# Decays by channel, a two-factor solve, wider MLP matmuls and a pacing scheduler in a fused RWKV-7 and MLP kernel

## The chip, the cores and the metric

One core of a Trainium2 chip runs the whole program. The metric is the device time of one execution in microseconds, as the median of several. Everything is fp32.

## The reference

A recurrence over 768 time steps for 4 batches of 8 heads of width 40, and an MLP on its output, with tokens as rows:

```python
for t in range(S):
    y[:, :, t] = np.einsum('bhd,bhde->bhe', rt, state)
    Sa = np.einsum('bhde,bhe->bhd', state, at)
    state_decay = state * wt[:, :, None, :] - np.einsum('bhd,bhe->bhde', Sa, bt)
    state = state_decay + np.einsum('bhd,bhe->bhde', vt, kt)
x = attn_out.transpose(0, 2, 1, 3).reshape(B * S, H * D)   # 3072 x 320
h = x @ w_in                                               # 320 -> 2048
g = h * (1.0 / (1.0 + np.exp(-1.702 * h)))
out = g @ w_out                                            # 2048 -> 320
```

`w_in` and `w_out` arrive as 64-bit floats and are converted in the kernel.

## The kernel before

**Units.** Time is cut into 12 chunks of 64 steps. A unit `i` is one chunk of two batches (16 heads), so there are 24 units; unit `i` needs the state that unit `i - 2` leaves. All matmuls work on quarters of the array: four 64x64 pieces, `QUARTERS`, each with its own 64 partitions of operands and of results. One `mm` in the code is one quarter, and an fp32 `mm` is two MATMUL and two LDWEIGHTS instructions in the profile.

**One unit.** `cum` multiplies the logarithms of the decays by triangles, which gives cumulative sums; `session` takes `Exp` of them (F, G and `wch`, and the `Ln` of the next chunk's decays, for two units at once). `prep` scales a, b and k by these, by time; `turned` transposes the three by matmuls with the identity (`ps_turn`, L487) and copies them back; the scores N, its transpose and A follow, each with a mask on VectorE, then A times v. `solve` adds the incoming state (`ah_z`, `ps_ahZ`) and solves (I - N) X = X0 in six levels (L592). A level holds W = [N | X | N transposed] for 16 heads in two halves b. Its matmuls square N, square its transpose, multiply X, and add X again by a matmul with the identity (L608); then one copy brings all from PSUM to the next W (L613). The last level keeps X alone. After it come the state's update (`ps_Z`), the transpose of the solution (`ps_saT`), the readout (`ps_rz`, `ps_M`, `ps_y`) and the transposed output xT (`ps_xT`), from which the MLP starts.

**The MLP.** For each chunk (256 tokens) `up` makes 8 tiles g of 256 hidden channels, 5 products of 256 columns each, with the activation on ScalarE; `down` makes two tiles of 128 tokens from 16 products of 320 columns each.

**PSUM.** Its eight banks are four pairs. Every group of matmuls takes a pair, and gives it back when its result has been read.

**Order.** Everything is a task of the class `Plan`, with a rank, its engines and their costs in ns, and what it reads and overwrites. `order` simulates the engines and writes out one order for all: of the tasks that are able to start, each engine takes the lowest rank. The recurrence has ranks around 10 i, the conversion of the weights 5000 and more, the MLP 10000 and more. `fits` says whether a PSUM pair is to be had: the MLP (`most=2`) may hold two and must leave one clear. `fetched` holds a model of instruction fetch on TensorE, 256 instructions in 3750 ns; where a task would wait over 100 ns for it, `order` looks for another task that would not. Each engine then executes its tasks in that order, and waits on semaphores. Buffers have the slots given at L198; a task that writes slot n waits for the users of the contents before.

Of the kernel before, what the change touches and what calls it, by code (L numbers as in the profile page):

```python
# [17 lines left out]
FP32 = mybir.dt.float32  # L18
# [37 lines left out]
class Plan:  # L56
# [4 lines left out]
    BLOCK, FETCH = 256, 3750.0  # L61
# [30 lines left out]
    def order(self):  # L92
# [84 lines left out]
def rwkv7_gelu_quick(ctx: ExitStack, tc: tile.TileContext, time_d, w_d, chan_d, w_in, w_out, out):  # L177
# [10 lines left out]
    LEVELS = 6  # L188
    HALF = [slice(0, 64), slice(64, 128)]
# [7 lines left out]

    plan = Plan(dict(in_w=4, logw=4, F=4, G=4, wch=4, wz=2, in_time=2, in_chan=3, kh=3, bh=3, ah=2,  # L198
                     ahT=2, khT=2, bhT=2, A=1, Av=2, RV=2, W=3, zraw=2, z=2, zT=2, sa=2, saT=1, M=1,
                     rz=1, y=1, x=2, xT=4, g=10, ob=1, raw=4, scale=2), 4)  # L200
# [49 lines left out]
    def triangle(name, compare, sign):  # L250

        t = single(name, [128, 64])
# [5 lines left out]
        return t  # L258


    incl = triangle("incl", ALU.is_ge, 1)
    excl = triangle("excl", ALU.is_gt, 1)
    halves = single("halves", [128, 2])
    nc.vector.memset(halves[:, 0:1], 0.0)
    nc.vector.memset(halves[:, 1:2], 1.0)
    for p in HALF:
        q = slice(p.start, p.start + MID)
        nc.vector.tensor_scalar_add(incl[q], incl[q], -1.0)
        nc.vector.tensor_scalar_add(excl[q], excl[q], -1.0)
        nc.vector.memset(halves[q, 0:1], 1.0)  # L270
        nc.vector.memset(halves[q, 1:2], 0.0)
    upper = triangle("upper", ALU.is_gt, 1)
    lower = triangle("lower", ALU.is_gt, -1)

    def mask(t):
# [3 lines left out]
    padded = {name: [single(f"{name}{i}", [128, 8, 64]) for i in range(plan.slots[name])]  # L279
              for name in ("kh", "bh", "ah", "z")}  # L280
    for ts in padded.values():
        for t in ts:
            nc.gpsimd.memset(t[:, :, D:], 0.0)
    sa = [single(f"sa{i}", [128, 2, 2, 2, 64]) for i in range(2)]
    for t in sa:
        nc.gpsimd.memset(t, 0.0)
    wch = [single(f"wch{i}", [128, 2, 2, 2, 2]) for i in range(4)]
    for t in wch:
        nc.vector.memset(t, 0.0)

    def kept(name, i):
        return padded[name][i % plan.slots[name]]
# [10 lines left out]
    def raws(n):  # L303
        q = n // 2
        if ("raw", q) not in tiles:
            tiles["raw", q] = work.tile([128, 2, DM], INT64, tag=f"xT{2 + q % 2}", name="raw")
        return tiles["raw", q][:, n % 2]

    def weight(n, key, dst, *srcs):
        P, cols = dst.shape  # L310
        rank = 5000 + n

        place = (n // 2) % 2
        raw = lambda: raws(n)[:P, :cols]
        word = lambda dt, w: raw().bitcast(dt).rearrange("p (n two) -> p n two", two=2)[:, :, w]
        scale = lambda: buf("scale", n, [128, 2, DM], INT32)[:P, 0, :cols]
        frac = lambda: buf("scale", n, [128, 2, DM], INT32)[:P, 1, :cols]

        def fetch(t):
            for i, src in enumerate(srcs):  # L320
                to = raw()[i * P // len(srcs):(i + 1) * P // len(srcs)]
                nc.sync.dma_start(to if len(src.shape) == 2 else
                                  to.rearrange("p (m f) -> p m f", m=src.shape[1]), src)
# [4 lines left out]
        def bounded(t):  # L328

            nc.gpsimd.tensor_scalar(scale().bitcast(FP32), scale().bitcast(FP32), low, high, ALU.max, ALU.min)  # L330
# [7 lines left out]
        def value(t):  # L338

            nc.vector.tensor_scalar(frac(), word(INT32, 1), 0xFFFFF, 0x100000, ALU.bitwise_and, ALU.bitwise_or)  # L340
            nc.vector.scalar_tensor_tensor(dst, in0=word(UINT32, 0), scalar=2.0 ** -32, in1=frac(),
                                           op0=ALU.mult, op1=ALU.add)
            nc.vector.scalar_tensor_tensor(dst, in0=dst, scalar=2.0 ** -20, in1=scale().bitcast(FP32),
                                           op0=ALU.mult, op1=ALU.mult)

        ns = 60.0 + 1.4 * cols
        here = dict(uses=[("xT", place - 2)])
        plan.add(15 + n * 0.4, {"SP": 60.0 * len(srcs)}, fetch, writes=[("raw", n)], size=P * cols * 8)
        plan.add(rank, {"DVE": ns}, magnitude, reads=[("raw", n)], writes=[("scale", n)], **here)
        plan.add(rank, {"POOL": 4.8 * cols}, bounded, reads=[("scale", n)], writes=[("bounded", n)])  # L350
        plan.add(rank, {"DVE": 2 * ns}, exponent, reads=[("raw", n), ("scale", n), ("bounded", n)], writes=[("exponent", n)], **here)
        plan.add(rank, {"DVE": 3 * ns}, value, reads=[("raw", n), ("scale", n), ("exponent", n)], writes=[key], **here)

    def weights():
        blocks = w_in.rearrange("(k p) (m r f) -> k r p m f", p=64, r=2, f=128)
        n = 0
        for m in range(0, NM, 2):
            for k in range(NK):
                weight(n, ("w_in", (m // 2, k)), w_in_sb[:, k, m:m + 2].rearrange("p m f -> p (m f)"),
                       blocks[k, 0][:, m:m + 2], blocks[k, 1][:, m:m + 2])  # L360
                n += 1
        for f in range(NF):
            weight(n, ("w_out", f), w_out_sb[:, f, :], w_out[f * 128:(f + 1) * 128, :])
            n += 1


    in_time = lambda i: buf("in_time", i, [128, 5, DM])
    in_chan = lambda i: buf("in_chan", i, [128, 2, 8, 64])
    in_w = lambda i: buf("in_w", i, [128, DM])
    logw = lambda i: buf("logw", i, [128, DM])  # L370

    def load_w(i):
        plan.add(10 * i - 20, {"SP": 60.0}, lambda t: nc.sync.dma_start(in_w(i), w_d[i]),
                 writes=[("in_w", i)], size=128 * DM * 4)

    def load(i):
        plan.add(10 * i, {"SP": 60.0}, lambda t: nc.sync.dma_start(in_time(i), time_d[i]),
                 writes=[("in_time", i)], size=128 * 5 * DM * 4)
        plan.add(10 * i, {"SP": 60.0}, lambda t: nc.sync.dma_start(in_chan(i), chan_d[i]),
                 writes=[("in_chan", i)], size=128 * 1024 * 4)  # L380
# [3 lines left out]
    G_of = lambda i: buf("G", i, [128, 2, 160])  # L384

    def cum(i):
        def go(t):
            ps, lw = psum(t, "ps_cum"), logw(i)
            for b in BITS:
                for n in BITS:  # L390
                    u = b ^ n
                    mm(ps[HALF[u], b, :160], incl[HALF[b]], lw[HALF[b], n * 160:(n + 1) * 160], True)
            for b in BITS:
                mm(ps[HALF[b], b, 160:480], excl[HALF[b]], lw[HALF[b]], False)
            for f in BITS:
                for n in BITS:
                    for b, e in QUARTERS:
                        u = b ^ n
                        o, h = 480 + 4 * u + 2 * f, head(e, f, b, u)
                        mm(ps[e * 64:e * 64 + D, b, o:o + 2], lw[HALF[b], h * D:(h + 1) * D], halves[HALF[b]], False)  # L400
        plan.add(10 * i - 9, pe((1, 160), (1, 320), (4, 2)), go, reads=[("logw", i)],
                 writes=[("cum", i)], room=[("F", i), ("G", i), ("wch", i)], pair=("cum", i))

    def session(c):

        now = [2 * c, 2 * c + 1] if c >= 0 else []
        nxt = [i for i in (2 * c + 2, 2 * c + 3) if i < NU]

        def exps(i):
            def go(t):  # L410
                if i == now[0]:
                    nc.scalar.preload_act_table_set("natural_log_exp_and_others")
                ps, w = psum(t, "ps_cum"), wch[i % 4]
                nc.scalar.activation(G_of(i), ps[:, :, :160], ACT.Exp, scale=-1.0)  # L414
                for b in BITS:
# [439 lines left out]
```

## Time and profile before

| | |
|---|---|
| median of 3 runs | 1110.31 us (1108.95 to 1114.78) |
| the profiled execution | 1109.09 us, its span 1107.4 us |
| TensorE busy, matmuls | 912.8 us, 32,416 MATMUL |
| VectorE / ScalarE / GpSimd busy | 319.1 / 366.4 / 81.5 us |
| costliest groups | `ps_up` 251.7 us, `ps_down` 232.8 us, `ps_level` 232.3 us and 121.2 us with the identity |
| first and last `ps_up` | 121.4 and 1085.3 us |
| first and last `ps_down` | 277.6 and 1102.4 us |
| last `ps_xT` of the recurrence | 947.4 us |

The busy time of the matmuls is the time in which at least one is in flight; four quarters run beside each other, and a matmul lasts longer than the distance to the next one. So a busy share says little of how full the array is; the number of MATMULs in a stretch of time says more.

### The profile page before, as it was taken

The page shows a single profiled execution, that of the slowest core. Times are in us where ns is not written, and L with a number is a line of the kernel's source. Part 1 is how long each engine was busy: PE and PEld are TensorE (multiplying, and loading weights), DVE is VectorE, ACT ScalarE, POOL GpSimd, SP SyncE. Part 2 cuts the span into 40 slices and gives each one's busy share as a digit, 9 for nine tenths or more (in the row PEclk, how much of TensorE's full clock was granted, in tenths as well). Part 3 has the DMA queues.
Part 4 walks back from the last instruction along what each step waited for, and adds up shares of the span by engine and source line. Part 5 has one row for each costly group of instructions (what it writes and reads, how often), then busy time and mean ns, then how long its engine had stood idle before and what let it go on. Part 6 is the DMA issues. An engine that isn't in the chain of part 4 may idle for free.

```text
span 1107.4 us, 67140 instructions
## 1 busy us (share of the span) xinstructions
PE 912.8 (82%) x32416; PEld 754.1 (68%) x32416; DVE 319.1 (29%) x688; ACT 366.4 (33%) x663; POOL 81.5 (7%) x115
## 2 busy tenths in 40 slices
PE   7566787756887777987768988688988999999998
PEld 6556676656676666777667867677877866666664
DVE  4686666322423224123132131320231200000000
ACT  4333433443335333243342344333244221111211
POOL 3322322100000000000010010000010000000000
PEclk8998989999999999999999999999999999999999
DMA  6333433201211011011111111201100000000000
GB/s 204 109 105 85 134 105 95 65 4 53 70 54 54 21 53 65 27 48 59 53 46 35 47 59 34 65 17 40 58 4 10 4 14 14 14 8 8 15 14 13
DMA packets 22542, 54.89 MB, mean 50 GB/s; under 512 B 2816, under 2 KB 14080, under 8 KB 22272
## 3 DMA queue, kind: packets, MB, share of 16 engines
q1 hardware_dynamic: 22272, 50.61, 14.8%
q8 instruction: 253, 4.15, 1.6%
q14 instruction: 17, 0.14, 0.0%
HBM read 46.66 MB, written 3.93 MB: 46 GB/s over the span
## 4 chain that ended last, share of the span: by engine, by line
PE 79%; issue 16%; DVE 2%; ACT 1%; DMA 0%; POOL 0%; SPq 0%; DVEq 0%; POOLq 0%; ACTq 0%
PE ps_up L739 19%; PE ps_down L758 19%; PE ps_level L219 18%; PE ps_turn L219 3%; PE ps_cum L219 2%; PE ps_y L219 2%; PE ps_N L219 2%; PE ps_Z L219 2%; PE ps_xT L219 1%; PE ps_saT L219 1%; PE ps_RV L219 1%; PE ps_Av L219 1%; PE ps_M L219 1%; PE ps_A L219 1%; PE ps_rz L219 1%
## 5 line engine op out<-in xcount | busy, mean ns | idle before, releaser
L219 PE MATMUL ps_level<-W 64*64 64x64 f32 (+2 forms) x8448 | 232.3, 236 | 61.3 <-issue 56.5
L219 PEld LDWEIGHTS ps_level<-W 64*64 64x64 f32 x8448 | 215.5, 137 | 77.4 <-issue 65.6
L739 PE MATMUL ps_up<-xT,w_in_sb 64*64 64x256 f32 x3840 | 251.7, 382 | 19.3 <-issue 17.2
L758 PE MATMUL ps_down<-w_out_sb,g 64*64 64x320 f32 x3072 | 232.8, 433 | 4.3 <-issue 4.1
L613 ACT COPY W<-ps_level 128x672 f32<-128x672 f32 (+1 forms) x220 | 148.7, 684 | 220.7 <-PE ps_level L219 214.2
L739 PEld LDWEIGHTS ps_up<-xT,w_in_sb 64*64 64x64 f32 x3840 | 160.5, 135 | 68.4 <-issue 28.6
L758 PEld LDWEIGHTS ps_down<-w_out_sb,g 64*64 64x64 f32 x3072 | 129.8, 134 | 70.4 <-issue 10.1
L219 PE MATMUL ps_level<-W,ident 64*64 64x80 f32 x2304 | 121.2, 238 | 8.2 <-issue 8.2
L745 ACT ACTIVATE g<-ps_up 128x512 f32<-128x512 f32 x96 | 57.4, 598 | 127.4 <-PE ps_up L739 126.4
L219 PEld LDWEIGHTS ps_level<-W,ident 64*64 64x64 f32 x2304 | 87.6, 138 | 10.2 <-issue 10.2
L769 DVE TENSOR_TENSOR ob<-ob,ps_down 128x320 f32<-128x320 f32 x24 | 11.7, 488 | 211.0 <-ACT ob L766 211.0
L766 ACT COPY ob<-ps_down 128x320 f32<-128x320 f32 x24 | 10.2, 426 | 127.5 <-PE ps_down L758 127.5
L330 POOL TENSOR_SCALAR scale<-scale 128x256 f32<-128x256 f32 (+1 forms) x36 | 41.3, 1160 | 116.0 <-DVE scale L326 116.0
L468 POOL TENSOR_TENSOR ah<-in_time,F 128x320 f32<-128x320 f32 x14 | 12.7, 904 | 360.5 <-ACT F L416 347.8
L473 POOL TENSOR_TENSOR kh<-in_time,G 128x320 f32<-128x320 f32 x18 | 16.6, 922 | 243.9 <-ACT G L414 146.2
L219 PE MATMUL ps_y<-kh,RV 64*64 64x40 f32 x768 | 28.8, 232 | 4.8 <-issue 4.8
L219 PE MATMUL ps_y<-bh,M 64*64 64x40 f32 x768 | 29.0, 235 | 4.0 <-issue 3.7
L613 DVE COPY W<-ps_level 128x416 f32<-128x416 f32 (+1 forms) x20 | 14.1, 709 | 63.1 <-PE ps_level L219 63.1
L219 PEld LDWEIGHTS ps_y<-kh,RV 64*64 64x64 f32 x768 | 27.4, 144 | 6.4 <-issue 5.2
L219 PE MATMUL ps_Z<-sa,bh 64*64 64x40 f32 x704 | 26.0, 226 | 4.1 <-issue 4.1
L219 PEld LDWEIGHTS ps_y<-bh,M 64*64 64x64 f32 x768 | 25.9, 145 | 4.6 <-issue 4.2
L508 DVE TENSOR_TENSOR W<-ps_N,upper 128x512 f32<-128x512 f32 x24 | 16.6, 691 | 42.7 <-PE ps_N L219 42.5
(113 smaller groups left out, 1111.8 us busy)
## 6 DMA issues: line engine op xcount, KB each, us to landing
in_time<-in_time SPq DMA_DIRECT2D x24, 800.0 KB, 4.6
in_chan<-in_chan SPq DMA_DIRECT2D x24, 512.0 KB, 4.3
raw<-in_w_in SPq DMA_DIRECT2D x40, 128.0 KB, 3.6
raw<-in_w_out SPq DMA_DIRECT2D x16, 320.0 KB, 3.7
in_w<-in_w SPq DMA_DIRECT2D x24, 160.0 KB, 3.4
out<-ob SPq DMA_DIRECT2D x48, 80.0 KB, 2.1
```

Source lines behind the costliest of these rows:

```text
L219: nc.tensor.matmul(o, lhsT, rhs, start=start, stop=True, skip_group_check=True)
L330: nc.gpsimd.tensor_scalar(scale().bitcast(FP32), scale().bitcast(FP32), low, high, ALU.max, ALU.min)
L468: plan.add(R, {"DVE": 490.0, "POOL": 900.0}, lambda t: of(t.engine).tensor_mul(ah[:, :, :D], by_head(in_time(i)[:, 3]), by_head(F_of(i))), ...
L473: plan.add(R, {"DVE": 490.0, "POOL": 900.0}, lambda t: of(t.engine).tensor_mul(kh[:, :, :D], by_head(in_time(i)[:, 0]), G()), reads=T("in_ ...
L508: plan.add(R + 1, dve(512), lambda t: nc.vector.tensor_tensor(W_of(6 * i).rearrange("p e b f n -> p e (b f) n")[:, :, :, o:o + 64], psum(t ...
L613: copy(t.engine)(W_of(s + 1)[:, :, b, :, lo:], view[:, :, :, lo:])
L739: nc.tensor.matmul(ph[HALF[h], r, :256], w_in_sb[HALF[r], k, m, h * 64:(h + 1) * 64], xT_of(j)[HALF[r], k, :], start=k == 0, stop=k == NK - 1)
L745: plan.add(10000 + 100 * j + m, act(512), lambda t, n=n: nc.scalar.activation(g_of(n), psum(t, "")[:, :, :256], ACT.Gelu_apprx_sigmoid), w ...
L758: nc.tensor.matmul(po[HALF[b], r, :DM], g_of(j * NM + m)[HALF[r], f % 2, o:o + 64], w_out_sb[HALF[r], f, :], start=f == 0, stop=f == NF - 1)
L766: copy(t.engine)(ob_of(n), psum(t, "")[:, 0, :DM])
L769: nc.vector.tensor_add(ob_of(n), ob_of(n), psum(t, "")[:, 1, :DM])
```

## The change

- **Decays by channel too.** The host sends a, k and b also by channel (`in_ak`, `in_b`), and r, v as before. `by_channel` multiplies the logarithms by both triangles at once and leaves the sums by channel (`ps_cumT`, 128 columns); `exp_channel` takes FT and GT from them. a, b and k are scaled by channel; the three transposes and their copies go. kh and bh by time are made beside that, for update and readout. `Exp` and its table load come once per unit, not per chunk.
- **N with the state.** b by channel and the state z lie side by side in `bz`, so that one matmul of 104 columns gives N and a times z.
- **The solve with I - P and I + P.** From unit 4 on (`EARLY`), level 0 writes W from an edge tile minus the result, and from then on a level multiplies by E = 2 I - P, which VectorE makes from PSUM beside the copy of W; the matmul with the identity goes. Units 0 to 3 use the old form up to level 4, and E = I + P in the last.
- **`sa_turned`** makes the transposed solution by matmuls from W and E beside the last level; before, it was made from the last level's result.
- **MLP.** `up` runs on two chunks (512 columns) at once in four of the eight groups, on one in the first two and last two; slots of g go from 10 of 256 columns to 8 of 512.
- **Weights.** They are converted in 10 + 8 pieces, before 20 + 16, and at ranks 8 to 17 instead of 5000.
- **The scheduler.** `fits` lets the MLP have one up pair and one down pair, and no longer keeps one clear. A matmul task that would bring TensorE over 300 ns ahead of the fetch gives way to another.

```diff
-    BLOCK, FETCH = 256, 3750.0
+    BLOCK, FETCH, AHEAD = 256, 3750.0, 300.0
...
-            return clear > 0 if t.most is None else clear > 1 and len(many) < t.most
+            return clear > 0 and (t.most is None or sum(k[0] == t.pair[0] for k in many) < t.most)
...
-        def wait(t):
-            return fetched(t, now)[0] - now - t.engines["PE"]
+        def ahead(t):
+            return (issued % self.BLOCK + t.instr) * self.FETCH / self.BLOCK - (now + t.engines["PE"] - begun)
...
-                    if took and e == "PE" and wait(took) > 100.0:
-                        took = next((t for t in able if e in t.engines and fits(t) and wait(t) <= 100.0), took)
+                    if took and e == "PE" and ahead(took) > self.AHEAD:
+                        took = next((t for t in able if e in t.engines and fits(t) and ahead(t) < min(self.AHEAD, ahead(took))), took)
...
+        def by_channel(t):
+            ps, lw = psum(t, "ps_cumT"), logw_of(i)
+            for u, f in product(BITS, BITS):
+                for b, e in QUARTERS:
+                    o, h = (2 * u + f) * 128, head(e, f, b, u)
+                    mm(ps[HALF[e], b, o:o + 128], lw[HALF[b], h * D:h * D + 64],
+                       both[HALF[b]].rearrange("p n t -> p (n t)"), o == 0)
...
-        turned("ahT", "ah", ahT)
-        turned("bhT", "bh", bhT)
-        turned("khT", "kh", khT)
...
             def go(t):
                 w, ps = W_of(s)[:, :, b], psum(t, "ps_level")
+                E = None if alone else E_of(es)[:, :, b]
...
-                        mm(ps[HALF[q], h, o + lo:o + 104], w[HALF[h], q, j, 104:], w[HALF[h], q, j, lo:104], j == 0)
+                        mm(ps[HALF[q], h, o + lo:o + 104], E[HALF[h], q, j, 64:] if E else w[HALF[h], q, j, 104:],
+                           w[HALF[h], q, j, lo:104], j == 0)
...
-                for h, q in QUARTERS:
-                    mm(view[HALF[q], h, :, 64:104], ident[HALF[h]], w[HALF[h], q, :, 64:104], False)
+                if alone:
+                    for h, q in QUARTERS:
+                        mm(view[HALF[q], h, :, 64:104], ident[HALF[h]], w[HALF[h], q, :, 64:104], False)
...
+                    plan.add(key, dve(512), lambda t: nc.vector.tensor_sub(
+                        E_of(es + 1)[:, :, b].rearrange("p h j (n t) -> p h (j n) t", n=2),
+                        wide(twice).to_broadcast([128, 2, 4, 64]), part(t)[:, :, :, :64]),
+                             writes=[(f"E{b}", es + 1), ("E", es + 1)], pair=pair)
+            if not last and (n or early):
+                plan.add(key, any2(4 * (168 - lo)), lambda t: copy(t.engine)(
+                    W_of(s + 1)[:, :, b, :, lo:], item(t)[:, :, :, lo:168]), writes=keeps, pair=pair)
...
+    groups = [[0], [1]] + [[c, c + 1] for c in range(2, NU // 2 - 2, 2)] + [[NU // 2 - 2], [NU // 2 - 1]]
```

More of the change, by code (lines that the diff above doesn't have):

```diff
@@ L343, in value @@
[L343 to L350, printed above, removed]
@@ new lines, in weight @@
+        one, two = 170.0 + 0.45 * cols, 150.0 + 1.07 * cols
+        plan.add(rank, {"SP": 60.0 * len(parts)}, fetch, writes=[(kind, n)], size=P * cols * 8, **here)
+        plan.add(rank, {"DVE": one}, magnitude, reads=[(kind, n)], writes=[("magnitude", key)], **here)
+        plan.add(rank, {"DVE": one, "POOL": 4.8 * cols}, bounded, reads=[("magnitude", key)], writes=[("bounded", key)], **here)
+        plan.add(rank, {"DVE": one}, significand, reads=[(kind, n)], writes=[("significand", key)], **here)
@@ L354, in weights @@
+        plan.add(rank, {"DVE": one + two}, exponent, reads=[("bounded", key)], writes=[("exponent", key)], **here)
+        plan.add(rank, {"DVE": 2 * two}, value, reads=[("significand", key), ("exponent", key)], writes=[key], **here)
     def weights():
         blocks = w_in.rearrange("(k p) (m r f) -> k r p m f", p=64, r=2, f=128)
[L356 to L370, printed above, removed]
+        for n, (m, k) in enumerate(product(range(0, NM, 4), range(NK))):
+            weight("wi", n, W_IN + 0.2 * n, ("w_in", (m // 4, k)), w_in_sb[:, k, m:m + 4].rearrange("p m f -> p (m f)"), w_in,
+                   [(HALF[r], blocks[k, r][:, m:m + 4]) for r in BITS])
@@ new lines, in weights @@
+        rows = w_out.rearrange("(n f p) d -> n p f d", p=128, f=2)
+        for n in range(NF // 2):
+            weight("wo", n, W_OUT + n, ("w_out", n), w_out_sb[:, 2 * n:2 * n + 2].rearrange("p f d -> p (f d)"), w_out,
+                   [(slice(0, 128), rows[n])])
+    time_of = lambda i: buf("time", i, [128, 4, DM])
+    ak_of = lambda i: buf("ak", i, [128, 2, 8, 64])
+    b_of = lambda i: buf("b", i, [128, 8, 64])
+    rv_of = lambda i: buf("rv", i, [128, 2, 8, 64])
+    logw_of = lambda i: logw_t[i % plan.slots["logw"]]
@@ new lines, in prep, with score_NT @@
+        for n, (name, dst) in enumerate((("kh", kh_of), ("bh", bh_of))):
+            plan.add(R + 4, {"POOL": 900.0, "DVE": 490.0}, lambda t, n=n, dst=dst: of(t.engine).tensor_mul(
+                dst(i)[:, :, :D], by_head(time_of(i)[:, n]), G()), reads=T("time", "exps", "G"), writes=T(name))
+        def score_NT(t):
+            ps = psum(t, "ps_NT")
+            for b, f in product(BITS, BITS):
+                for e, u in QUARTERS:
+                    o, j = (2 * b + f) * 64, slot(b, u, f)
+                    mm(ps[HALF[u], e, o:o + 64], bz_of(i)[HALF[e], j, :64], ahT()[HALF[e], j], o == 0)
@@ L517, in score_A @@
+        plan.add(R + 1, pe((4, 64)), score_NT, reads=T("bhT", "ahT"), uses=T("bz", "ak"), room=[("W", 6 * i)], pair=("NT", i))
+        plan.add(R + 1, dve(512), lambda t: nc.vector.tensor_tensor(
+            W_of(6 * i).rearrange("p e b f n -> p e (b f) n")[:, :, :, 104:],
+            psum(t, "")[:, :, :256].rearrange("p e (j t) -> p e j t", t=64), mask(upper), ALU.mult),
+                 writes=[("W", 6 * i)], pair=("NT", i))
         def score_A(t):
@@ L587, in solve @@
+            plan.add(R + 5, pe((4, 40)), state_turned, reads=T("z", "bhT"), uses=T("bz"), room=T("zT"), pair=("zT", i))
             plan.add(R + 5, any2(320), lambda t: copy(t.engine)(
@@ L589, in solve @@
         else:
[L590 removed]
+            plan.add(R, any2(320), lambda t: copy(t.engine)(first()[:, :, :, 64:104], Av()), reads=T("Av"), writes=[("W", 6 * i)])
         def level(n, b):
[L594 to L595 removed]
+            last = n == LEVELS - 1
+            early = i < EARLY
+            alone = n == 0 or early and not last
@@ L748, in down, with mlp, up, go @@
-    def down(j):
-        for p in range(2):
-            n = 2 * j + p
-            def part(m, p=p, n=n):
+    def mlp(n, chunks):
+        R = 10000 + 100 * n
+        N = 256 * len(chunks)
+        first = chunks[0] % 2 * 256
+        def up(m, k):
+            def go(t):
+                ph, x = psum(t, "ps_up"), xT_of(chunks[0] // 2)[:, k, first:first + N]
+                for r, h in QUARTERS:
+                    nc.tensor.matmul(ph[HALF[h], r, :N], w_in_sb[HALF[r], k, m, h * 64:(h + 1) * 64], x[HALF[r]],
+                                     start=k == 0, stop=k == NK - 1)
+            plan.add(R + m, pe((1, N)), go, reads=[("xs", (c, p)) for c in chunks for p in BITS] + [("w_in", (m // 4, k))],
+                     uses=[("xT", chunks[0] // 2)], room=[("g", n * NM + m)], pair=("up", n * NM + m), most=1)
+        def gelu(m):
+            plan.add(R + m, act(2 * N), lambda t: nc.scalar.activation(
+                g_of(n * NM + m)[:, :, :N], psum(t, "")[:, :, :N], ACT.Gelu_apprx_sigmoid),
+                     writes=[("g", n * NM + m)], pair=("up", n * NM + m))
+        def down(i, c, p):
+            serial = 2 * c + p
+            def part(m):
```

549 lines of the change are left out of this document (272 added, 277 removed).

## The prediction

> **What bounds the kernel now.** I read the page first (sections 1 to 4), then the waits, then the timeline of the matrix engine, then the windows by stage. In the page's rows, PE is the matmul, PEld the weight load; the digits are tenths of 40 slices of 27.7 us.
>
> ```profile
> span 1107.4 us, 67140 instructions
> PE 912.8 (82%) x32416; PEld 754.1 (68%) x32416; DVE 319.1 (29%) x688; ACT 366.4 (33%) x663; POOL 81.5 (7%) x115
> PE   7566787756887777987768988688988999999998
> GB/s 204 109 105 85 134 105 95 65 4 53 70 54 54 21 53 65 27 48 59 53 46 35 47 59 34 65 17 40 58 4 10 4 14 14 14 8 8 15 14 13
> q8 instruction: 253, 4.15, 1.6%
> PE 79%; issue 16%; DVE 2%; ACT 1%; DMA 0%; POOL 0%; SPq 0%; DVEq 0%; POOLq 0%; ACTq 0%
> ```
>
> The chain is matmuls plus "issue", in which the engine waited for nothing that the profile shows; DVE and ACT end 3% of it. What issue is, the instruction queue tells: 32,416 MATMULs and as many weight loads are 64,832 instructions, and 253 packets carried them, so a packet holds 256. The PE timeline shows them arriving:
>
> ```profile
> 440.10 0.43 PE L739 MATMUL ps_up<-xT,w_in_sb 64*64 64x256 f32 x2 [0.53 <-issue]
> 443.57 0.43 PE L739 MATMUL ps_up<-xT,w_in_sb 64*64 64x256 f32 x2 [0.21 <-issue]
> 450.51 0.43 PE L739 MATMUL ps_up<-xT,w_in_sb 64*64 64x256 f32 x2 [0.21 <-issue]
> ```
>
> The stalls are 3.47 us apart (once twice that, 6.94), whatever stands between. So PE has two limits: the fetch, and the streaming of columns. Windows of PE alone (us, busy, MATMULs, clock, DMA share, GB/s); first all MATMULs. The last row is the fullest of twenty equal stretches, with all engines' columns (the first x is the MATMULs):
>
> ```profile
> 0.00:110.70 110.70, 73.08 (x3284) 0.91 0.42 126
> 221.50:775.20 553.70, 439.38 (x18371) 0.98 0.15 45
> 775.20:885.90 110.70, 99.41 (x3432) 1.00 0.07 19
> 941.30:1052.00 110.70, 110.70 (x1923) 1.00 0.05 11
> 664.40:719.80 55.40, 41.93 (x1920) 39.34 (x1914) 15.06 (x30) 21.93 (x41) 1.35 (x3) 1.00 0.16 50
> ```
>
> Per MATMUL with its load: 33.7 ns at the start, 30.14 in the long middle, 28.9 at best. Only after 886 us is it 57 ns at a busy share of 100%: there the MLP alone is left, and streaming binds. Its share in the middle, ups and then downs, for the second and third of those stretches:
>
> ```profile
> 221.50:775.20 553.70, 83.06 (x1056) 0.98 0.15 45
> 775.20:885.90 110.70, 36.95 (x584) 1.00 0.07 19
> ```
> ```profile
> 221.50:775.20 553.70, 91.06 (x1056) 0.98 0.15 45
> 775.20:885.90 110.70, 28.61 (x360) 1.00 0.07 19
> ```
>
> So by 775 us not a third of the 3,072 downs has run: while the fetch binds, the columns are idle; when the columns bind, the fetch is.
>
> The prices of a streaming MATMUL come from the longest pieces of the chain, and for small ones from a stretch that PE ran without a stall:
>
> ```profile
> 1033.87 17.27 PE ps_up L739 x320
> 1085.63 17.27 PE ps_down L758 x256
> ```
> ```profile
> 30.18 0.25 PE L219 MATMUL ps_level<-W 64*64 64x104 f32 x1
> 31.64 0.22 PE L219 MATMUL ps_N<-ahT,bhT 64*64 64x64 f32 x1
> 463.77 0.64 PE L219 MATMUL ps_ahZ<-z,ahT 64*64 64x40 f32 x32
> ```
> ```profile
> L219 PE MATMUL ps_ahZ<-z,ahT 64*64 64x40 f32 x704 | 16.7, 227 | 5.8 <-issue 5.8
> ```
>
> An up of 256 columns costs 54.0 ns, a down of 320 67.5 (0.211 ns a column). Between the second and third row lie 80 level MATMULs in 1.46 us, 18.2 ns each; 32 narrow ones start within 0.64 - 0.227 us, 13.3 ns each. All are below the 28.9 of the fetch: each small MATMUL is paid for by its instructions, not its columns.
>
> **The change, part by part.** *Matmuls.* Counted from the code, each `mm` being two MATMULs and two weight loads. Before: 538 `mm` in a unit. The three transposes go (-48), as the time operands now arrive by channel; `ps_ahZ` becomes 40 more columns of `score_N` (-16); levels 1 to 4 lose the identity product and level 5 too (-40, from unit 4 on; only -8 in units 0 to 3); cum stays at 22. That leaves 434, in units 0 to 3 466. Less what the first and last two units lack, this is 10,416 `mm`, 20,832 MATMULs. MLP up over two chunks in four of eight groups: 3,840 become 2,560 of the same columns in all; downs stay 3,072. Sum 26,464, 18% fewer. Fetch alone: 26,464 x 28.9 = 765 us at best, x 30.14 = 798.
>
> *Columns.* 9,088 level MATMULs x 18.2 = 165 us; 9,920 of 40 to 64 columns x 13.5 = 134; 768 of 104 and 768 of 128 by the column price 37; 288 of `by_time`, half the array in part, some 19. Together 355, 17.1 ns each. The MLP: 3,840 x 54.0 + 3,072 x 67.5 = 414, unchanged. Sum 769 us. So fetch and columns become equal, 765 to 798 against 769, and all hangs on how well they run at once.
>
> *Pacing.* The old rule takes MLP only where the next block is late by over 100 ns; the new one whenever PE is over 300 ns ahead of the fetch. How it mixes no row shows. The nearest is 775.20 to 885.90, where both kinds ran: columns 584 x 54.0 + 360 x 67.5 + 2,488 x 16.0 (the old mean of a small one, rival 4) = 95.7 of 110.7 us, 86%, and fetch 3,432 x 28.9 = 99.2, 90%. That is one bound; the other is mixing without loss.
>
> *Weights.* Before, the last conversions and the first MLP matmuls are (first and last start):
>
> ```profile
> L343 DVE SCALAR_TENSOR_TENSOR w_out_sb<-w_out_sb,scale x16: 491/492/1029, 115.5 to 192.6; 128x320 f32<-128x320 f32 x16
> L758 PE MATMUL ps_down<-w_out_sb,g x3072: 427/429/740, 277.6 to 1102.4; 64*64 64x320 f32 x192
> L739 PE MATMUL ps_up<-xT,w_in_sb x3840: 372/376/683, 121.4 to 1085.3; 64*64 64x256 f32 x192
> ```
>
> The conversion moves from behind everything (rank 5000) to ranks 8 to 17, ahead of unit 1's solve on SP, DVE and POOL. In 18 larger pieces, five vector operations or six, I estimate 71 to 85 us on DVE, as now. It can delay units 1 to 3, whose cover is their level copies on ACT; I put ups at about 70 us and downs near 110.
>
> *Loads.* A unit brings 2.13 MB for 1.50, in five issues for three. At the first slice's 204 GB/s the first two units land 6 us later, but `ak` comes first: +4 us. Later the 15 MB more lie under a mean of 45 GB/s: nothing, unless packets slow the fetch (the start's 33.7 ns against 30.14, at 126 GB/s).
>
> *DVE and ACT.*
>
> ```profile
> L508 DVE TENSOR_TENSOR W<-ps_N,upper 128x512 f32<-128x512 f32 x24 | 16.6, 691 | 42.7 <-PE ps_N L219 42.5
> L613 DVE COPY W<-ps_level 128x672 f32<-128x672 f32 x9 | 7.6, 855 | 13.2 <-PE ps_level L219 13.1
> L613 ACT COPY W<-ps_level 128x672 f32<-128x672 f32 x183 | 130.0, 719 | 174.4 <-PE ps_level L219 170.7 <-issue 1.3 <-DVE xT L723 1.2
> L412 ACT ACT_TABLE_LOAD x12 | 15.4, 1283 | 0.2
> ```
>
> A late unit's levels put on DVE 2 x (855 + 691) ns, 6 x 691 and two small ones, 8.1 us, and the rest of its vector work some 7: with the weights 430 us of 860, half. ACT gains up to 25 table loads x 1.283 = 32 us, loses copies of transposes: near 400. Both stay under the columns. The longer ACT session of each unit (two `Exp` groups and a table load, some 5 us) holds up the level copies queued behind it; DVE may take those, so I take 0, with 32 us as upper end.
>
> *The sum.* Start: units 0 to 3, 3,600 MATMULs x 33.7 = 121, + 4, with 24 us of MLP columns already in it. Middle: 17,232 MATMULs of recurrence x 17.1 + (414 - 24 - 34.5) of MLP = 650 us of columns; 756 at 86%. By fetch, some 21,850 x 30.14 = 659. New pacing stops neither engine for long stretches, as the old does, so I take halfway between 659 and 756, 707. Tail: the last chunk's MLP, 2 x 17.27 = 34.5; after the last matmul 5 (1102.4 to 1107.4). 125 + 707 + 34.5 + 5 = 872. The profiled execution took 1109.09 us beside its span of 1107.4, and the median of the three runs shown, 1110.31, is 1.2 above it: 874.
>
> The Trainium skill ("Runtime: NRT & Kernel Launch", Instruction fetch mechanics) has the 16 KiB blocks of 256 instructions too, but calls crossing a block "mostly hidden". The trace disagrees by its stalls 3.47 us apart; by that rule only columns would count, and the sum would be rival 4's.
>
> **The rivals.**
> 1. *The mixing stays as it was.* Against it: weights are ready before the old 192.6 us. For it: MLP may hold only one up and one down pair, and 300 ns is little. At the middle's share, 2,112 MLP MATMULs beside 16,259, the 17,232 take 587 us and do 136 us of MLP; 254 us are left. 125 + 587 + 254 + 5 = 971.
> 2. *Two readers of one pair.* In levels 1 to 4 DVE takes E and ACT takes W from the same pair. The planner lets them run at once. The trace shows no such pair; the only two readers of one, `ob`, go in turn:
>
> ```profile
> DVE ob L769 <- ACT ob L766: 211.0, 23, 25.4
> ```
> In turn, each level is 0.69 us longer; the two halves overlap, so 4 x 0.69 x 20 units = 55 us if PE, whose order is fixed, waits each time: 927. With MLP queued ahead of the level it is partly hidden. The Trainium skill ("PSUM — Partial Sum Buffer", PSUM bank collisions raise a hardware error) has ScalarE and VectorE reads of one bank collide, so that they have to be ordered; no run here shows it. By that page the sum is this rival's.
> 3. *No loss in mixing,* and a start at the middle's pace: 3,600 x 30.14 = 108 + 650 + 34.5 + 5 = 798.
> 4. *The fetch does not bind.* Then only columns fall. The recurrence had 10,752 level MATMULs x 18.2 + 14,752 x 13.5, and some 14 for the wide ones of cum, 409 us (16.0 each); it has 355: 1107 - 54 = 1053. Against it: the 16% of issue.
> 5. *Slower: the PSUM pairs bind.* Up and down may hold two of four pairs nearly always (`clear > 0` drops the spare). A unit uses 26 pairs; with two left, its period is 13 times the mean hold. It costs more than now if 20 units fill 1107 - 164 = 943 us, 47 each, a mean hold of 3.6 us. By the rows a level holds 32 x 30.14 = 0.96 + 0.72 + 0.69 = 2.4 with some wakeups, the two decays about 5. So it needs every hold to be half as long again.
>
> **How the numbers follow.** Forecast (820 to 910, DVE, ACT and loads at their ends included) 0.54; rival 1 (915 to 1000) 0.18; rival 2 (900 to 935) 0.15; rival 3 (under 815) 0.06; rival 4 0.02; rival 5 0.05. The runs spread over 0.5% (1108.95 to 1114.78), so 0.5% is what can be told. Only rival 5 is slower, 0.05; 0.02 of 1 and 4 drift to no change; faster 0.93. The likeliest case's own range is 820 to 910; the range for 8 in 10 is 805 to 965.
>
> **What would show it.** x26464 MATMULs and about 207 instruction packets; no `ps_turn`, `ps_ahZ`; ups x2560, a double one near 107 ns when streaming; the first up near 70 us, the first down near 110; the digits of PE 9 in the middle, not only at the end, and 50 to 70 small MATMULs between two ups; a last transposed x about 50 us before the end. The forecast is wrong if ups and downs again crowd the last 200 us (1), if PE waits for `W` or E on DVE or ACT in the levels (2), if the windows show both busy shares low (5), or if the time per MATMUL in the middle leaves 29 to 33 ns.

## The result and the profile after

The changed kernel takes 957.9 us (957.24 to 959.27) against 1111.5 us, 0.862 of the time before (95% interval 0.859 to 0.865); a second comparison gave 958.3 us and 0.868 (0.865 to 0.872). Forecast were 874 us in a range of 805 to 965. The kernel before took 1104 to 1112 us in the comparisons below, the changed one 958 twice; so times are given beside the ratios.

The page after, the lines that answer to those of before:

```profile
span 957.4 us, 55394 instructions
PE 843.7 (88%) x26464; PEld 629.3 (66%) x26464; DVE 478.1 (50%) x820; ACT 334.2 (35%) x604; POOL 125.1 (13%) x124
PE   5675779899766888999999999899799998999998
PEclk9875979999999989999999999999999999999999
q8 instruction: 207, 3.39, 1.5%
PE 74%; DVE 11%; issue 7%; ACT 6%; DMA 1%; POOL 0%; SPq 0%; ACTq 0%; DVEq 0%; POOLq 0%
```

The instructions are those counted: 26,464 MATMULs in 207 packets. Issue fell from 16% of the chain to 7%, and VectorE and ScalarE, 3% before, now make up 17% of it. From a third of the span on the digits are 8 and 9, but for one 7, where before they ran from 6 to 9 up to three quarters of the span. The start did not gain. In windows (all engines at first: us, PE, PEld, DVE, ACT, POOL, granted clock, DMA share, GB/s; then PE alone, last the ups and the downs of the same stretch):

```profile
0.00:47.90 47.90, 28.95 (x1048) 25.24 (x1052) 25.52 (x56) 21.59 (x39) 14.83 (x30) 0.91 0.66 208
47.90:95.70 47.80, 31.39 (x1104) 28.47 (x1100) 41.64 (x69) 14.13 (x30) 19.95 (x14) 0.68 0.52 156
95.70:143.60 47.90, 36.33 (x1127) 29.85 (x1123) 40.43 (x68) 15.55 (x28) 19.41 (x9) 0.84 0.40 113
143.60:800.00 656.40, 596.98 (x19464) 0.99 0.21 66
```
```profile
143.60:800.00 656.40, 178.98 (x1596) 0.99 0.21 66
```
```profile
143.60:800.00 656.40, 166.50 (x2064) 0.99 0.21 66
```

VectorE is 86% busy from 48 to 144 us, while TensorE gets some 1,100 MATMULs in 48 us. The kernel before has 1,402 in the second of these windows:

```profile
47.90:95.70 47.80, 31.12 (x1402) 28.74 (x1403) 32.75 (x83) 16.04 (x31) 12.83 (x14) 0.86 0.38 118
```

From 143.6 to 800 us, called the middle from here on, there is one MATMUL per 33.7 ns. A double up (512 columns) costs what was forecast from its columns (24 in 2.58 us, 107.5 ns):

```profile
758.26 2.58 PE ps_up L783 x24
```

So in the middle the columns were used for 464 single ups x 54.0 + 1,132 double x 107.5 + 2,064 downs x 67.5 + 15,804 others x 17.1 ns = 556 of 656 us, 85%; before, from 221 to 775 us, 1,056 x 54.0 + 1,056 x 67.5 + 16,259 x 16.0 = 388 of 554, 70%. The fetch at its best, 28.9 ns, would be used to 86%.

### The profile page after: what moved, and what is told of

Its sections match the earlier page's. It is cut to its first block, busy times and chain, and to the rows that moved or that the text cites. A ratio compares the mean times of both kernels' runs of the same rounds, so it can differ in the third digit from the quotient of the medians.

```text
span 957.4 us, 55394 instructions
## 1 busy us (share of the span) xinstructions
PE 843.7 (88%) x26464; PEld 629.3 (66%) x26464; DVE 478.1 (50%) x820; ACT 334.2 (35%) x604; POOL 125.1 (13%) x124
## 4 chain that ended last, share of the span: by engine, by line
PE 74%; DVE 11%; issue 7%; ACT 6%; DMA 1%; POOL 0%; SPq 0%; ACTq 0%; DVEq 0%; POOLq 0%
PE ps_down L802 21%; PE ps_up L783 20%; PE ps_level L222 14%; ACT W L652 3%; DVE E L647 2%; PE ps_Z L222 2%; PE ps_cumT L222 2%; PE ps_y L222 2%; PE ps_N L222 2%; PE ps_cum L222 2%; PE ps_xT L222 2%; PE ps_A L222 1%; PE ps_saT L222 1%; PE ps_rz L222 1%; PE ps_Av L222 1%
## 5 line engine op out<-in xcount | busy, mean ns | idle before, releaser
L783 PE MATMUL ps_up<-xT,w_in_sb 64*64 64x256 f32 (+1 forms) x2560 | 250.9, 493 | 1.4 <-ACT W L652 0.6
L652 ACT COPY W<-ps_level 128x672 f32<-128x672 f32 (+1 forms) x171 | 106.3, 629 | 226.9 <-PE ps_level L222 174.1
L222 PEld LDWEIGHTS ps_level<-W,E 64*64 64x64 f32 x5888 | 135.3, 136 | 73.6 <-issue 27.8
L222 PE MATMUL ps_level<-W,E 64*64 64x64 f32 (+2 forms) x5888 | 143.7, 234 | 27.4 <-ACT W L652 6.9
L647 DVE TENSOR_TENSOR E<-twice,ps_level 128x512 f32<-128x512 f32 x120 | 80.2, 685 | 83.2 <-ACT W L652 64.3
L783 PEld LDWEIGHTS ps_up<-xT,w_in_sb 64*64 64x64 f32 x2560 | 90.4, 136 | 34.6 <-issue 16.1
L789 ACT ACTIVATE g<-ps_up 128x512 f32<-128x512 f32 (+1 forms) x64 | 51.9, 811 | 118.6 <-PE ps_up L783 118.2
L222 PEld LDWEIGHTS ps_level<-W 64*64 64x64 f32 x2560 | 67.7, 142 | 25.3 <-issue 16.3
L222 PE MATMUL ps_level<-W 64*64 64x64 f32 (+2 forms) x2560 | 70.8, 244 | 13.6 <-issue 10.0
L632 DVE TENSOR_TENSOR W<-edge,ps_level 128x672 f32<-128x672 f32 x40 | 34.1, 853 | 34.8 <-PE ps_level L222 33.8
L642 DVE TENSOR_TENSOR E<-twice,ps_level 128x256 f32<-128x256 f32 x40 | 16.7, 419 | 28.9 <-ACT W L652 18.9
```

The source lines that it names most:

```text
L222: nc.tensor.matmul(o, lhsT, rhs, start=start, stop=True, skip_group_check=True)
L632: plan.add(key, dve(672), lambda t: nc.vector.tensor_sub(W_of(s + 1)[:, :, b], wide(edge).to_broadcast([128, 2, 2, 168]), item(t)[:, :, :, ...
L642: plan.add(key, dve(256), lambda t: nc.vector.tensor_tensor(E_of(es + 1)[:, :, b, :, 64:], wide(ident if early else twice).to_broadcast([1 ...
L647: plan.add(key, dve(512), lambda t: nc.vector.tensor_sub(E_of(es + 1)[:, :, b].rearrange("p h j (n t) -> p h (j n) t", n=2), wide(twice).t ...
L652: plan.add(key, any2(4 * (168 - lo)), lambda t: copy(t.engine)(W_of(s + 1)[:, :, b, :, lo:], item(t)[:, :, :, lo:168]), writes=keeps, pair ...
L783: nc.tensor.matmul(ph[HALF[h], r, :N], w_in_sb[HALF[r], k, m, h * 64:(h + 1) * 64], x[HALF[r]], start=k == 0, stop=k == NK - 1)
```

## The experiments

### The old scheduling rules, and the new ones alone

```diff
-            return clear > 0 and (t.most is None or sum(k[0] == t.pair[0] for k in many) < t.most)
+            return clear > 0 if t.most is None else clear > 1 and len(many) < 2
...
-                    if took and e == "PE" and ahead(took) > self.AHEAD:
+                    if took and e == "PE" and wait(took) > 100.0:
```

> The changed kernel with the two scheduling rules of before: the MLP may hold two PSUM pairs of any kind and must leave one clear, and it is chosen only where the next instruction block would be late by over 100 ns. The changed kernel takes 957.9 us. Theory A (the pacing does mix fetch and columns, and what misses to the forecast is lost elsewhere): the mixing falls back to the middle of the kernel before, so MLP is left for the end: my rival of 971 was worked out with a start of 125 us, and the start takes some 30 us more, so 990 to 1030, with over 150 us after the last transposed output. Theory B (the pacing brought little, the missing 85 us are its failure): 945 to 975, same tail as now, some 76 us.

Measured 1034.2 us, 0.936 (0.932 to 0.941): 76 us more than the changed kernel. Its last transposed x, and then the changed kernel's, first and last start:

```profile
L225 PE MATMUL ps_xT<-ident,x x960: 216/218/366, 43.7 to 862.8; 64*64 64x64 f32 x192
```
```profile
L222 PE MATMUL ps_xT<-ident,x x960: 213/218/367, 43.4 to 881.3; 64*64 64x64 f32 x192
```

The recurrence ends 19 us earlier, and 167 us of MLP stand after it (span 1030.3), where the changed kernel has 76. In its middle the columns are used to 73% (560 x 54.0 + 640 x 107.5 + 1,448 x 67.5 + 16,480 x 17.1 = 479 of 656 us), near the 70% of the kernel before:

```profile
143.60:800.00 656.40, 549.48 (x19128) 0.96 0.20 65
```

Theory A holds, just over the upper end of its range.

The same rules put into the kernel before (the edit in the other direction):

> The kernel before with nothing but the two new scheduling rules (one up and one down pair, none kept clear; over 300 ns ahead of the fetch gives way). It keeps its 32,416 MATMULs and the late weights. Theory A (pacing alone recovers the columns that lay idle while the fetch bound): fetch 32,416 x 29 to 30.1 ns = 940 to 977, plus a tail of 35 to 70 us: 1000 to 1045. Theory B (the pacing only pays once the instructions are fewer): 1080 to 1110. With old_scheduler (0.936 of before) this tells whether the two halves of the change add or multiply.

Measured 1024.3 us, 0.928 (0.924 to 0.933), theory A. All MATMULs of its middle, then its ups and downs:

```profile
143.60:800.00 656.40, 596.26 (x21777) 0.97 0.16 47
```
```profile
143.60:800.00 656.40, 180.81 (x2560) 0.97 0.16 47
```
```profile
143.60:800.00 656.40, 175.76 (x2156) 0.97 0.16 47
```

30.1 ns a MATMUL, the same as in the middle before, but with 2,560 x 54.0 + 2,156 x 67.5 + 17,061 x 16.0 = 557 us of columns, 85% and no longer 70%. The rows of waits in this window say what still stops it: of the 60 us in which no matmul is in flight, 54 are put down to issue, which the prediction traced to the fetch; in the changed kernel it is 28 of 59, and most of the rest are waits for VectorE and ScalarE. (In the same window of the kernel before, issue had 128 us.) The product 0.936 x 0.928 = 0.869, or the sum of the two gains, 1 - 0.064 - 0.072 = 0.864, is about the ratio of the whole change (0.862 and 0.868): two halves of like size, and whether they add or multiply these intervals do not tell.

### The old solve

```diff
-    EARLY = 4
+    EARLY = 24
```

> EARLY = 24: all units solve in the old form, with the matmul with the identity up to level 4 and no E but in the last level. 1,280 MATMULs more (27,744; 40 x 2 in each of 20 units less what the last level saves), at 28.9 to 30.1 ns 37 us if the fetch binds throughout. But levels 1 to 3 have one reader of a PSUM pair again, the copy, and VectorE loses 7 us a unit. Theory A (two readers in turn, which the planner does not know of, cost about 55 us): the gain outweighs the cost, 930 to 955. Theory B (readers in turn are hidden by other units' work): 975 to 1000. Near 958 the two would just cancel.

969.5 us, 0.877 (0.873 to 0.880): some 11 us more than the changed kernel. It lies between the theories, below the 37 us of B and above A's gain, so the solve with I - P and I + P is worth a little. It fits that its second reader takes back a part of what its matmuls save; the next runs size that part.

### Two readers of one PSUM pair

The waits of the changed kernel (us in all, times, longest; E is made at L647, W copied at L652):

```profile
DVE E L647 <- ACT W L652: 64.3, 52, 4.8
ACT W L652 <- DVE E L647: 39.7, 31, 3.2
PEld ps_level L222 <- ACT W L652: 13.1, 20, 1.1
PEld ps_level L222 <- DVE E L647: 11.1, 23, 1.0
```

The readers wait for each other, as rival 2 said, and TensorE for them, which the planner did not foresee. Three edits ask what it costs. First, the planner is told:

```diff
-            t.after.update(o for o in writers if "PE" in o.engines)
+            t.after.update(writers)
```

> The planner is told that readers of one PSUM pair go in turn: each task on a pair follows all tasks on it that were added before, not only the matmuls. Nothing is computed differently; the orders change. Theory A (a fixed order made for parallel readers stalls TensorE): 925 to 950, and TensorE's waits for W and E in the levels shrink to less than half. Theory B (the longer chain itself is the cost, whoever plans it): 950 to 965. Theory C (hidden anyway): no change, 953 to 963, as the waits seen are no loss.

941.6 us, 0.853 (0.849 to 0.856), 16 us less. Theory A by its time, but not by its sign. TensorE's waits for E in the levels are gone (28 us before, 1 now, rows of weight loads and matmuls added), as E is now read first; those for the copy did not shrink. Together its waits for W and E fell from 57 to 32 us, not to less than half.

```profile
PEld ps_level L222 <- ACT W L652: 13.5, 19, 1.8
```

The order moved as well: the last transposed x starts at 836.0 us in place of 881.3. Second, the turn is taken away:

```diff
-                        wide(twice).to_broadcast([128, 2, 4, 64]), part(t)[:, :, :, :64]),
-                             writes=[(f"E{b}", es + 1), ("E", es + 1)], pair=pair)
+                        wide(twice).to_broadcast([128, 2, 4, 64]),
+                        E_of(es)[:, :, b].rearrange("p h j (n t) -> p h (j n) t", n=2)),
+                             uses=[("E", es)], writes=[(f"E{b}", es + 1), ("E", es + 1)], pair=pair)
```

> The changed kernel, but in levels 1 to 3 of units 4 to 23 VectorE makes E from the level's own E in place of the matmuls' result: an instruction of the same size that reads no PSUM. The solve's result is thereby another one; all matmuls, copies and vector operations stay in number and size. It takes away the turn of the two readers and E's wait for the matmuls. The changed kernel: 958 us. Theory A (the readers in turn stall TensorE's fixed order): 915 to 940. Theory B (they are covered by other work and the missing time lies in the start and in PSUM pairs): 948 to 962.

934.3 us, 0.842 (0.840 to 0.845): 24 us less, theory A. So much the turn, with E's wait for the matmuls, costs in the changed kernel (the order changes a little with the edit too). The gain lies in the middle, where the columns are now used to 88% (440 x 54.0 + 1,220 x 107.5 + 2,064 x 67.5 + 16,564 x 17.1 = 577 of 656 us). Rival 2's 55 us took every level's wait as uncovered. Third, halves by bank:

```diff
+                    def factor(h):   # E from bank h
+                        plan.add(key, dve(256), lambda t: nc.vector.tensor_sub(
+                            E_of(es + 1)[:, h, b].rearrange("p j (n t) -> p (j n) t", n=2),
+                            twice.unsqueeze(1).to_broadcast([128, 4, 64]), part(t)[:, h, :, :64]), ..., side=h)
+                    def kept(h):     # W from bank h
+                        plan.add(key, any2(2 * (168 - lo)), lambda t: copy(t.engine)(
+                            W_of(s + 1)[:, h, b, :, lo:], item(t)[:, h, :, lo:168]), ..., side=h)
+                    factor(0); kept(1); factor(1); kept(0)
...
+            t.after.update(o for o in writers if "PE" in o.engines or None in (o.side, side) or o.side == side)
```

> Like readers_in_turn, but in levels 1 to 3 E and W are each read in two halves by bank: VectorE takes E of bank 0 while the copy of W takes bank 1, then they change sides; the planner knows it. By the rows a level's reading is 2 x max(0.42, 0.47) us in place of 0.69 + 0.72, some 0.5 us shorter, for 240 more instructions of VectorE or ScalarE of about 0.2 us overhead each. Theory A (the turn of the two readers is on the path that sets the recurrence's pace): 10 us or more below readers_in_turn, 0.835 to 0.845 of before. Theory B (once the order knows of it, other work covers it): 0.848 to 0.858 of before.

952.9 us, 0.864 (0.860 to 0.869): 11 us above readers_in_turn, neither theory. The timeline of one level shows why:

```profile
402.83 0.44 ACT L656 COPY W<-ps_level 128x336 f32<-128x336 f32 x1 [4.61 <-PE ps_level L224]
403.30 0.42 DVE L650 TENSOR_TENSOR E<-twice,ps_level 128x256 f32<-128x256 f32 x1 [0.73 <-ACT W L656]
403.76 0.44 ACT L656 COPY W<-ps_level 128x336 f32<-128x336 f32 x1 [0.49 <-DVE E L650]
404.23 0.42 DVE L650 TENSOR_TENSOR E<-twice,ps_level 128x256 f32<-128x256 f32 x1 [0.51 <-ACT W L656]
```

All four go in turn, 1.8 us and not 1.0, each released by the other engine's half, though the two read different banks. So the built program seems to order the readers of the whole tile of a pair, not of its banks; a version with a tile for each bank wasn't tried.

### The weights at the start

```diff
-    W_IN, W_OUT = 8, 10
+    W_IN, W_OUT = 28, 30
```

> W_IN, W_OUT = 28, 30 in place of 8, 10: the weights' conversion gets the rank of units 3 and 4, behind the solves of units 1 and 2. In the changed kernel VectorE is 85% busy from 48 to 144 us and TensorE has only 1,100 MATMULs per 48 us there, at a clock of 0.68 in one stretch. Theory A (conversion ahead of the recurrence starves it): the first two chunks end 15 to 20 us earlier and the whole takes 935 to 948. Theory B (VectorE has to do this work before the MLP can start, whatever the order; the MLP then starts later by as much): 953 to 963.

945.0 us, 0.853 (0.849 to 0.857), 13 us less; the window from 47.9 to 95.7 us holds 1,473 MATMULs for 1,104. Theory A by its time; the first two chunks end 12 us earlier, not 15 to 20. The third ends no earlier, which fits that the conversion still has to be done.

The weights' work itself cut, so that the kernel leaves out most of the conversion and computes with other weights:

```diff
-            of(t.engine).scalar_tensor_tensor(dst, in0=dst, scalar=2.0 ** -20, in1=scale().bitcast(FP32),
-                                              op0=ALU.mult, op1=ALU.mult)
...
-        plan.add(rank, {"DVE": one}, magnitude, ...)
-        plan.add(rank, {"DVE": one, "POOL": 4.8 * cols}, bounded, ...)
...
-        plan.add(rank, {"DVE": one + two}, exponent, ...)
-        plan.add(rank, {"DVE": 2 * two}, value, reads=[("significand", key), ("exponent", key)], writes=[key], **here)
+        plan.add(rank, {"DVE": two}, value, reads=[("significand", key)], writes=[key], **here)
```

> The changed kernel with two vector operations for each piece of the weights in place of six or seven (the significand and one multiply-add); magnitude, bounds and exponent are left out, so the weights are not the right ones. VectorE's work on them falls from 72 to some 23 us, the loads stay. Theory A (VectorE is what holds the start back): the first two chunks end 20 to 30 us earlier, at 935 to 945 in all, about what weights_late gave or a little less. Theory B (the loads or the recurrence's own chain hold the start): 952 to 960, first chunk within 5 us of now.

934.6 us, 0.842 (0.839 to 0.846): 23 us less, theory A, though its first two chunks end only 14 and 18 us earlier, not 20 to 30. Its window from 47.9 us, then that of weights_late, against the second row of the changed kernel's:

```profile
47.90:95.70 47.80, 37.40 (x1347) 33.01 (x1345) 25.72 (x43) 17.87 (x35) 5.85 (x6) 0.85 0.48 147
```
```profile
47.90:95.70 47.80, 36.43 (x1473) 32.29 (x1470) 43.05 (x69) 21.61 (x40) 18.34 (x13) 0.92 0.48 143
```

With less to convert VectorE falls from 41.6 to 25.7 us, GpSimd from 20.0 to 5.9, and TensorE rises by 243 MATMULs; with the recurrence first, VectorE is as busy as in the changed kernel and TensorE has 369 more.

### Does the fetch still bind?

```diff
-    groups = [[0], [1]] + [[c, c + 1] for c in range(2, NU // 2 - 2, 2)] + [[NU // 2 - 2], [NU // 2 - 1]]
+    groups = [[c] for c in range(NU // 2)]
```

> All 12 groups of the MLP take one chunk, so every up has 256 columns: 1,280 MATMULs more (27,744), the same columns, and 32 more activations of 512 elements for 32 fewer of 1,024. Theory A (the fetch binds in the middle): + 1,280 x 29 to 30 ns = 37 us, 985 to 1000. Theory B (with pacing the columns and the recurrence's own chain bind, and the MLP's instructions ride along): 945 to 970.

Beside it ran the changed kernel once more:

> The changed kernel as it is, on the chip of the three others, for comparison: 945 to 960.

962.2 us, 0.872 (0.868 to 0.877), beside 958.3 us, 0.868 (0.865 to 0.872): 4 us for 1,280 MATMULs, not 37, and the intervals overlap. Theory B. In the middle it has one MATMUL per 32.8 ns:

```profile
143.60:800.00 656.40, 600.19 (x20035) 0.98 0.21 63
```

The planner's price of a block, on top of the edit of readers_in_turn:

```diff
-    BLOCK, FETCH, AHEAD = 256, 3750.0, 300.0
+    BLOCK, FETCH, AHEAD = 256, 3500.0, 300.0
```

> readers_in_turn (942 us) with the planner's time per instruction block at 3,500 ns in place of 3,750, nearer to the stalls 3.47 us apart. Theory A (the pacing takes MLP too often, since the fetch is faster than it believes): 920 to 935. Theory B (as fetched blocks are 4.0 us apart in the middle, with loads and waits between, the model is right or kind already): 940 to 955.

949.3 us, 0.856 (0.853 to 0.859). By time that is 8 us above readers_in_turn; by the ratios (0.856 and 0.853, intervals overlapping) a loss is not clear, but no gain is there. Theory B:

```profile
L222 PE MATMUL ps_xT<-ident,x x960: 212/218/311, 43.7 to 805.4; 64*64 64x64 f32 x192
```

The recurrence ends 31 us earlier than in readers_in_turn, as the planner believes that it may issue more, and 141 us of MLP remain. An earlier end of the recurrence alone is no gain.

### The fixes together

```diff
-            t.after.update(o for o in writers if "PE" in o.engines)
+            t.after.update(writers)
...
-    W_IN, W_OUT = 8, 10
+    W_IN, W_OUT = 38, 40
...
-    BLOCK, FETCH, AHEAD = 256, 3750.0, 300.0
+    BLOCK, FETCH, AHEAD = 256, 3600.0, 200.0
```

> The fixes together: readers in turn known to the planner, weights at ranks 38 and 40, 3,600 ns a block, 200 ns ahead. If the gains add (958 - 16 - 13 - up to 10): 915 to 930. If they overlap, since the weights and the readers want the same VectorE: 930 to 942.

936.1 us, 0.843 (0.840 to 0.846): 22 us below the changed kernel, the fastest of those that leave out or change nothing of the computation. That is the second theory: the gains do not add in full. 16 and 13 became 22, whatever the two numbers of the planner did.

## Why the prediction was right, and where its terms were off

The direction and the range held; the sum was 85 us short of the span (872 for 957.4), and the number came out nearer to rival 1's 971 than to the forecast. Yet rival 1's mechanism is not what happened: the columns are used to 85%, not 70%, and old_scheduler shows how it would look, with 73%, 167 us of MLP at the end and 1034 us. The likeliest case's own range, 820 to 910 us, was missed; the wide range held by 7 us, with an upper end that the rivals had widened, not the losses that came. That much of it was luck.

Time in which columns lie idle gives the two terms that were mis-sized. The first and last MLP matmuls, for what follows:

```profile
L783 PE MATMUL ps_up<-xT,w_in_sb x2560: 372/589/1091, 99.3 to 941.5; 64*64 64x256 f32 x99, 64*64 64x512 f32 x98
L802 PE MATMUL ps_down<-w_out_sb,g x3072: 426/429/793, 110.5 to 952.2; 64*64 64x320 f32 x192
```

- **The start.** Forecast: 125 us with 3,600 x 17.1 + 24 = 86 us of columns, 39 idle. Measured to 143.6 us: 3,055 x 17.1 + 176 x 54.0 + 48 x 67.5 = 65, 79 idle: 40 us of the 85 (the border of 143.6 us is a choice). The step that failed is that of the weights: "It can delay units 1 to 3, whose cover is their level copies on ACT", priced at nothing. The levels have that cover; the masks, the products that make z and x, and the state updates have only VectorE, and the conversion had the better rank. light_weights takes back 23 us in all, some 13 of them here (3,648 x 17.1 + 200 x 54.0 + 64 x 67.5 = 78 us of columns to 143.6 us, for 65). Idle columns are not all: by the three windows the clock was granted in full for 89 us and at half for some 55, and 65 us of columns spread evenly would take 25 us longer by it (an estimate; in the row from which the start was forecast the clock was 0.91). The last section has the rows. The first up came at 99.3 us, not near 70; the first down at 110.5, as said.
- **The middle.** Forecast, with the tail: 741.5 us for 684.5 of columns, 57 idle. Measured from 143.6 to the last matmul at 952.2: 809 us for 769 - 65 = 704, 105 idle: 48, the rest and a little more, as the sums are rounded. The step that failed is the halving: "New pacing stops neither engine for long stretches, as the old does, so I take halfway". The bound taken from 775 to 886 us, 86%, was nearly the value itself. The turn of rival 2 has a part of up to 24 us in this (e_not_from_psum).

Up to about half of the 85 us is thus sized by runs that take one cause away; whether 23 and 24 would add was not run. The rest is open: in the middle three kernels of different instruction counts (the changed one, scheduler_alone, and single_chunk_up with 2,728 x 54.0 + 2,256 x 67.5 + 15,051 x 17.1 = 557 us) use 85% of the columns. In scheduler_alone TensorE's pauses are nearly all for issue; in the other two half of them are waits for VectorE and ScalarE, and what makes these come to the same 85% is not shown. Fewer PSUM pairs for the recurrence, the mechanism of rival 5, would be one cause; no run took it apart.

Point by point: MATMULs and packets exactly; columns 107.5 ns for a double up, as worked out; the fetch, which I had equal to the columns, no longer sets the pace (33.7 ns, outside the 29 to 33 that I named as a sign, and single_chunk_up); the tail was two chunks, 76 us, not one. ScalarE has 40 table loads for 23 (17 x 1.283 = 22 us, up to 32 were allowed for), but is busy for 334 us, below the 400 forecast; VectorE came to 478, above the 430. Of the signs that the forecast is wrong two were seen: the time per MATMUL, and TensorE waiting for W and E in the levels (rival 2), at up to 24 us and not 55.

Three readings of rows in the prediction were off. The wait of `ob` was no evidence for two readers in turn: VectorE adds to the `ob` that ScalarE has just written, so the data alone put it second; the turn itself is shown by the rows of E and W above. The 1,056 downs that had run by 775 us are a little over a third of 3,072, not less. And the 80 level MATMULs lie between the first and the second row of their view. Neither of the last two changes a term.

The Trainium skill ("PSUM — Partial Sum Buffer", PSUM bank collisions raise a hardware error) wants readers on ScalarE and VectorE ordered where they share a bank. The trace agrees that they go in turn, and shows them in turn on different banks too, which that page does not ask for.

## What to carry to other kernels

Where one limit binds in one stage and another in the next, running the two stages at once can be worth as much as taking work away: here each gave about 7%, and the two together about the whole 13 to 14%. Once the first limit no longer binds, taking away more of it does little (here 1,280 MATMULs, their columns kept, for 4 us). Telling the plan of the order a wait that the built program has was worth 16 us without any other edit; an order in which the recurrence merely ends earlier was not. Work moved forward to start a later stage sooner is to be costed on the engine that the first stage has no substitute for.

## What was not expected of the hardware

The granted clock fell to 0.68 between 48 and 96 us in the changed kernel, in a stretch in which TensorE waited up to 4.9 us at a time, and was 0.85 and 0.92 in the same window of light_weights and weights_late (the column after the engines in their rows). Its longest waits there:

```profile
PEld ps_rz L222 <- DVE y L747: 4.9, 1, 4.9
PEld ps_RV L222 <- issue: 4.1, 1, 4.1
```

In windows of 1 us from 44 to 98 us the clock is 1.00 or 0.50, and in between only where it changes. It falls three times:

```profile
46.00:47.00 1.00, 0.00 (x0) 0.63 0.93 183
70.00:71.00 1.00, 0.87 (x36) 0.58 0.53 126
83.00:84.00 1.00, 0.00 (x0) 0.91 0.22 82
```

No matmul was in flight from 45.3 to 47.2, from 67.8 to 69.3 and from 81.8 to 85.8 us. The Trainium skill ("TensorE: Matmul & The Clock Gate", HAM oscillation) has pauses over 3.4 us lower the clock. The trace agrees for the third fall at most, which comes 2 us into a pause of 4.0 us; the first two stand at pauses of 1.8 and 1.5 us. So shorter pauses, or the thin work around them, lowered it here too; no run takes the two apart.

What it costs is seen on one level of a unit of the old form: 80 MATMULs took 1.46 us at full clock in the kernel before, and here, at 0.50, nearly twice that:

```profile
93.84 2.77 PE ps_level L222 x80
```

A thin start is so paid for twice.
